# A planned recurrent-attention and gated-MLP kernel: transfers planned in a row, 48-column states, an update of eight products

## The chip, the core and the metric

The kernel runs on one core of a Trainium2 chip. Five engines work side by side and meet through semaphores: PE (TensorE: matmuls, with the weight loads listed apart as PEld), DVE (VectorE), ACT (ScalarE), POOL (GpSimd) and SP, which here does nothing but issue DMA transfers. The metric is the device time of one execution in microseconds; the figure of a kernel is the median of its runs.

## The reference

Four batches of eight heads carry a 48x48 state through 768 steps; the outputs of all heads side by side, 384 numbers for each of 3072 tokens, then go through a gated MLP of 2048 hidden units.

```python
for t in range(S):
    state = alpha[:, :, t, :, None] * state + np.einsum('bhd,bhe->bhde', k[:, :, t], v[:, :, t])
    y[:, :, t] = np.einsum('bhd,bhde->bhe', q[:, :, t], state)
...
h = x @ w_in
sp = np.where(h > 20.0, h, np.log1p(np.exp(np.minimum(h, 20.0))))
g = h * np.tanh(sp)
return (g @ w_out).astype(np.float32)
```

All inputs and the output are float32.

## The kernel before

**Attention.** `attention(n)` (L420 to L667) treats one chunk: 128 tokens of one batch, all eight heads. There are 24 chunks, the four batches in turn for each of six stretches of the sequence, so that chunk n and chunk n+4 share a state. Heads go in four pairs j; the two heads of a pair lie on partitions 0 to 47 and 64 to 111 of q, k and alpha (`R` is 112). DVE makes running products of alpha from the back (`rest`, L471) and from the front (L483) and multiplies them into k (L479) and q (L493). PE then makes the scores of the chunk (`sc`, L507, eight products with 48 rows of weights each), DVE masks them into `probs` (L515), and PE sums in `y` what the state gives (L530, `state` as weights) and what the chunk itself gives (L530, `v` as weights). ACT and DVE split `y` into an upper and a lower fp32r half (`xs`, and `x3` for the last two heads, whose rows six small DMAs then move into place, L576). For the next chunk of the batch PE turns k round (`kb`, L638), ACT copies it (`ks`, L642), PE multiplies it with v (`u`, L647), and DVE adds the diagonal blocks of `u` into the state (L659), which it has decayed first (L498).

The state of a batch holds for each pair a 112x112 block-diagonal tile, with zeros off the diagonal, so one product serves both heads of a pair. Decay and addition touch the two diagonal blocks in two instructions each. The update product makes all 96 columns of a pair, of which half the entries are used.

**MLP.** `unit` (L673 to L796) treats one block f of 128 hidden units for two or four chunks: nine products to `h` (L689), eight passes over 256 or 512 columns on ACT and DVE (L697 to L723) to `g`, and three products per chunk into an output bank `o` (L753). There are 110 units. `weight` unpacks the weights of a block with three DVE passes over `w_lead` (L340, L345, L350) and splits them into `wi` and `wo`; `weight_check` loads every block a second time (`wc`).

**Order.** Nothing of this is ordered by a scheduler: `Plan.order` plays all tasks through with the costs of `COST` and due times (keys), and emits them in that order under a manual schedule. A key is counted in units. A chunk is due `LEAD` units before the first unit that needs it, and at least `SPREAD` units before the next chunk; the weights of block f are due `W_LEAD` units ahead, shifted by `W_SHIFT`. A transfer is a task of SP (some row moves: of ACT) with a time to issue and a fixed time until it has landed, whatever else is in flight. The first `PARTED` chunks load alpha apart from q and k. Until 24 us of the plan, `fill` puts products of 384 columns that nobody reads (`spare`, L804) where the plan sees PE idle. Only what comes before and after the plan, such as the last check on `ok`, `every` and `pf` (L842 to L866), is placed by the framework's own scheduler. After it each engine reads the flag `good` and jumps over the code of `general_path`.

Of the kernel before, what the change touches and what calls it, by code (L numbers as in the profile page):

```python
# [9 lines left out]
F32 = mybir.dt.float32  # L10
F32R = mybir.dt.float32r
BF16 = mybir.dt.bfloat16
I32 = mybir.dt.int32
U32 = mybir.dt.uint32
AF = mybir.ActivationFunctionType
ALU = mybir.AluOpType
# [34 lines left out]
LEAD = 8.0  # L51
SPREAD = 2.0
W_LEAD = 4.0
# [5 lines left out]
CHECK_STEP = 2.0  # L59
FILLS = 150  # L60
IDLE, IDLE_UNTIL, IDLE_BANK = 12.34567, 24.0, "o3"
EARLY_BANKS = {0: ["att", "att", "o0", "o1", "o0"], 1: ["o2", "o1", "att", "o0", "o1"]}
PARTED = 3
DUE_SHIFT = {}
W_SHIFT = {5: -2, 7: -2, 15: -1}
X_PE = 4
# [17 lines left out]
class Task:  # L84
    def __init__(self, engine, cost, late, key, emit, port):
        self.engine, self.cost, self.late, self.key, self.emit = engine, cost, late, key, emit
        self.port = port
        self.needs, self.behind, self.uses, self.begin = [], [], [], None


class Plan:


# [10 lines left out]

    def add(self, engine, cost, late, key, emit, needs=(), uses=(), behind=(), port=False):
        t = Task(engine, cost, late, key, emit, port)
        t.needs, t.uses, t.behind = list(needs), list(uses), list(behind)
# [18 lines left out]
    def order(self):  # L126
# [6 lines left out]
        for e in ENGINES:  # L133
            waiting[e].sort(key=lambda t: t.key)
        done, n, port_free = [], len(self.tasks), 0.0

# [23 lines left out]
        while len(done) < n:  # L160
# [48 lines left out]
COST = {  # L209
    "load part": (0.7, 3.3), "load q": (1.8, 5.0), "load two": (1.2, 4.0), "load v": (0.7, 4.0),  # L210
    "load w": (2.0, 5.0),
    "move": (0.63, 2.5), "store": (0.47, 3.0),
    "fill": (0.165, 0.2), "fill0": (0.33, 0.36),
# [19 lines left out]


def fast_path(ctx, tc, qka, v, w, out, good):
    nc = tc.nc
# [85 lines left out]
    def weight(f):  # L322
# [9 lines left out]

        got = add("SP", *COST["load w"], max(key, FIRST_W + f) - 4, load, uses=[stage])
        fs = slice(f * P, (f + 1) * P)
# [53 lines left out]
    def weight_check(f):  # L388
# [20 lines left out]

        t = add("SP", *COST["load w"], key - 4, load, uses=[again])  # L410
        t = add("ACT", *COST["w check"], key, squares, [t], [again])
# [8 lines left out]
    def attention(n):  # L420
# [27 lines left out]
        if n == 0:  # L448
            got_a, got_k, got_q = (
                add("SP", *COST["load part"], -99 + 0.1 * i, load_part(*e), uses=[q_buf])  # L450
                for i, e in enumerate(((a_at, QKA), (k_at, a_at), (0, k_at)))
            )
        elif n < PARTED:
            got_a, got_k = (
                add("SP", *COST[z], key - Q_LEAD - early, load_part(*e), uses=[q_buf])
                for z, e, early in (
                    ("load part", (a_at, QKA), 1.0), ("load two", (0, a_at), 0.0)
                )
            )
            got_q = got_k  # L460
        else:
            got_a = got_k = got_q = add("SP", *COST["load q"], key - Q_LEAD, load, uses=[q_buf])
        got_v = add("SP", *COST["load v"], key - V_LEAD, load_v, uses=[v_buf])

# [29 lines left out]

        def decay(r):
            def part():
                o = st[r : r + D, :, r : r + D]
                nc.vector.tensor_tensor(  # L498
                    o, o, total()[r : r + D].broadcast_to([D, NPAIR, D]), ALU.mult
                )  # L500
            return part

# [15 lines left out]
        def product():  # L518
            p = new(y_buf, [P, NPAIR, C], f"y{n}", ps)
            ops = []  # L520
            if not first:
                ops += [(p[:R, j], st[:, j], Q()[:, j]) for j in range(NPAIR)]
            for j in range(NPAIR):
# [5 lines left out]
            for m, (o, l, r) in enumerate(ops):  # L529
                nc.tensor.matmul(  # L530
                    o, l, r, start=m < (2 if first else 1), stop=m >= len(ops) - 2,
                    skip_group_check=True,
                )
# [60 lines left out]
        if not first:  # L594
            for i, r in enumerate((0, 64)):
                t_decay.append(
                    add(
                        "DVE", *COST["state"], key + 0.1, decay(r), [t_rest, *done_state[b]],
                        [rest], port=True,
                    )  # L600
                )
        t_sc = add("PE", *COST["scores"], key + 0.2, scores, [t_k, t_q], [q_buf, *sc_buf])
        t_mask = [
# [21 lines left out]
        moved = [  # L625
            add(MOVER(n, s, r), *COST["move"], key + 0.64, move(s, r), [hi3, lo3, hi, lo], [x3])
            for s in range(NK) for r in (0, 64)
# [16 lines left out]
        def update():  # L644
            p = new(u_buf, [P, NPAIR, C], f"u{n}", ps)
            for j in range(NPAIR):
                nc.tensor.matmul(  # L647
                    p[:R, j, : 2 * D], ks_buf.tile[:, j], V()[:, 2 * D * j : 2 * D * (j + 1)],
                    start=True, stop=True,
                )  # L650

        def gather(a, r):
            def part():
                o = st[r : r + D, :, r : r + D]
                u = u_buf.tile[r : r + D, :, a * D : (a + 1) * D]
                if first:
                    nc.scalar.copy(o, u)
                else:
                    nc.vector.tensor_tensor(o, u, o, ALU.add)  # L659
            return part  # L660
# [4 lines left out]
        done_state[b] = [  # L665
            add(
                *(("ACT", *COST["state0"]) if first else ("DVE", *COST["state"])), key + 1.0,  # L667
                gather(a, r), [t_u, t_y, *t_decay], [u_buf],
            )
            for a, r in enumerate((0, 64))  # L670
        ]

# [3 lines left out]
    def unit(c0, nt, f, at, ends):  # L676
# [64 lines left out]
        for j in range(nt):  # L741
# [51 lines left out]
            written = add("ACT", *COST["result"], k, result, done, [osb] if from_part else [o, osb])  # L793
            add("SP", *COST["store"], k, store, [written], [osb])

# [67 lines left out]
    nc.vector.memset(ones, 1.0)  # L863
    pf = ps.tile([1, 3 + n_chunks - n_last], F32, tag="att", name="pf", bufs=BUFS["att"])
    nc.tensor.matmul(pf, ones, every, start=True, stop=True)
    nc.vector.tensor_reduce(good, pf, AX.X, ALU.min)  # L866
# [196 lines left out]
```

## Time and profile before

| what | us |
|---|---|
| median of three runs | 536.36 |
| the three runs | 536.14, 536.36, 539.34 |
| the profiled execution, its own time | 539.41 |
| its span, first to last instruction | 537.6 |

The profile is of a fourth execution. Its span leaves out 1.8 us around the program, and the execution took 0.6% more than the median of the runs; durations below come from it, and the comparison of kernels goes by the medians. In the rows, a `MATMUL` of plain float32 is two instructions, one of fp32r is one, so the four update products of a chunk are eight rows of `u`. A timeline row gives start, length, engine, line, operation, tiles and count; neighbouring instructions of one group stand in one row. Matmuls overlap each other, so the time that a group takes on PE is read from the start of its row to the start of the next. A bracket at a row's end tells how long the engine was idle before it, and who ended that.

### The profile page before, as it was taken

The page shows a single profiled execution, that of the slowest core. Times are in us where ns is not written, and L with a number is a line of the kernel's source. Part 1 is how long each engine was busy: PE and PEld are TensorE (multiplying, and loading weights), DVE is VectorE, ACT ScalarE, POOL GpSimd, SP SyncE. Part 2 cuts the span into 40 slices and gives each one's busy share as a digit, 9 for nine tenths or more (in the row PEclk, how much of TensorE's full clock was granted, in tenths as well). Part 3 has the DMA queues.
Part 4 walks back from the last instruction along what each step waited for, and adds up shares of the span by engine and source line. Part 5 has one row for each costly group of instructions (what it writes and reads, how often), then busy time and mean ns, then how long its engine had stood idle before and what let it go on. Part 6 is the DMA issues. An engine that isn't in the chain of part 4 may idle for free.

```text
span 537.6 us, 9425 instructions
## 1 busy us (share of the span) xinstructions
PE 524.9 (98%) x3392; PEld 467.2 (87%) x3392; DVE 394.3 (73%) x686; ACT 397.4 (74%) x930; POOL 36.0 (7%) x37
## 2 busy tenths in 40 slices
PE   7998999999999999999999999999999999999996
PEld 4688998998898888988899888899988899999996
DVE  8998999999997598678875567885458745554452
ACT  1597787899789797998676855567776577787774
POOL 2003010332440000000000000000000000000000
PEclk9999999999999999999999999999999999999999
DMA  8685243532533668556120132220042000010001
GB/s 262 193 267 176 75 134 83 183 119 65 178 118 121 190 191 268 203 176 199 51 68 1 44 90 75 75 73 1 1 132 76 7 9 1 0 60 1 1 0 62
DMA packets 22067, 54.18 MB, mean 101 GB/s; under 512 B 4033, under 2 KB 14785, under 8 KB 22017
## 3 DMA queue, kind: packets, MB, share of 16 engines
q1 hardware_dynamic: 21728, 53.45, 31.9%
q8 instruction: 27, 0.44, 0.4%
q14 instruction: 24, 0.19, 0.1%
q10 hardware_dynamic: 288, 0.10, 0.1%
HBM read 46.45 MB, written 4.72 MB: 95 GB/s over the span
## 4 chain that ended last, share of the span: by engine, by line
PE 74%; DVE 12%; DMA 6%; ACT 5%; issue 2%; SPq 1%; DVEq 0%; ACTq 0%
PE o L753 30%; PE h L689 30%; PE y L530 7%; PE sc L507 4%; DMA ws<-in_wp_dram 3%; PE u L647 2%; DVE w_lead L345 2%; DVE t L716 2%; PE kb L638 1%; DVE rest L471 1%; DVE g L723 1%; DMA qka<-in_qka_dram 1%; DVE w_lead L350 1%; DVE y L707 1%; DMA xs<-x 1%
## 5 line engine op out<-in xcount | busy, mean ns | idle before, releaser
L753 PE MATMUL o<-wo,g 128*128 128x384 f32 x1152 | 229.2, 342 | 0.6 <-DVE g L723 0.6
L689 PE MATMUL h<-xs,wi 128*128 128x512 f32 (+1 forms) x990 | 219.2, 366 | 0.7 <-DMA xs<-x 0.7
L753 PEld LDWEIGHTS o<-wo,g 128*128 128x128 f32 x1152 | 201.8, 188 | 10.2 <-DVE g L723 1.2
L689 PEld LDWEIGHTS h<-xs,wi 128*128 128x128 f32 x990 | 170.1, 188 | 26.7 <-DMA xs<-x 0.9
L697 ACT ACTIVATE u<-h 128x512 f32<-128x512 f32 (+1 forms) x110 | 59.3, 539 | 86.8 <-PE h L689 86.6
L707 DVE SCALAR_TENSOR_TENSOR y<-u,h 128x512 f32<-128x512 f32 (+1 forms) x110 | 67.4, 615 | 54.2 <-ACT u L697 53.8
L723 DVE TENSOR_TENSOR g<-t,g 128x512 fp32r<-128x512 f32 (+1 forms) x110 | 68.9, 627 | 50.4 <-ACT g L720 50.1
L710 ACT ACTIVATE t<-t,tenth 128x512 f32<-128x512 f32 (+1 forms) x110 | 73.2, 665 | 2.2
L716 DVE SCALAR_TENSOR_TENSOR t<-y,t 128x512 f32<-128x512 f32 (+1 forms) x110 | 69.4, 632 | 4.4 <-ACT t L713 4.4
L720 ACT ACTIVATE g<-t 128x512 fp32r<-128x512 f32 (+1 forms) x110 | 62.4, 567 | 8.2 <-DVE t L716 4.4
L703 ACT ACTIVATE t<-u 128x512 f32<-128x512 f32 (+1 forms) x110 | 63.3, 575 | 5.3 <-DVE g L723 1.9
L713 ACT ACTIVATE t<-t 128x512 f32<-128x512 f32 (+1 forms) x110 | 62.5, 568 | 0.6
L471 DVE TENSOR_TENSOR_SCAN rest<-qka,behind 112x516 f32<-112x516 f32 x24 | 30.3, 1262 | 10.1 <-DMA qka<-in_qka_dram 10.1
L515 DVE COPY_PREDICATED probs<-causal,sc 128x512 f32<-128x512 uint32 x48 | 32.5, 728 | 0.4 <-PE sc L507 0.2
L507 PEld LDWEIGHTS sc<-qka 48*128 48x128 f32 x384 | 23.6, 187 | 8.0 <-issue 3.1
L483 DVE TENSOR_TENSOR_SCAN qka<-qka,ahead 112x516 f32<-112x516 f32 x24 | 30.2, 1259 | 0.0
L507 PE MATMUL sc<-qka 48*128 48x128 f32 x384 | 28.2, 285 | 2.0 <-DVE qka L493 2.0
L366 POOL TENSOR_TENSOR wi<-w_lead,wi 128x384 fp32r<-128x384 f32 x12 | 18.8, 1570 | 122.1 <-ACT wi L363 122.1
L530 PE MATMUL y<-probs,v 128*64 128x128 f32 (+1 forms) x384 | 26.6, 278 | 0.1
L530 PEld LDWEIGHTS y<-probs,v 128*64 128x64 f32 (+1 forms) x384 | 20.5, 129 | 4.1 <-DVE probs L515 1.0
L530 PE MATMUL y<-qka,state 112*112 112x128 f32 x160 | 20.9, 273 | 0.8 <-DVE probs L515 0.8
L697 ACT ACTIVATION_READ_ACCUMULATOR u<-h 128x1 f32 x110 | 21.4, 194 | 0.0
(82 smaller groups left out, 381.9 us busy)
## 6 DMA issues: line engine op xcount, KB each, us to landing
qka<-in_qka_dram SPq DMA_DIRECT2D x21, 674.2 KB, 4.8
ws<-in_wp_dram SPq DMA_DIRECT2D x16, 768.0 KB, 4.6
wc<-in_wp_dram SPq DMA_DIRECT2D x16, 768.0 KB, 4.8
v<-in_vp_dram SPq DMA_DIRECT2D x24, 192.0 KB, 3.4
out_dram<-osb SPq DMA_DIRECT2D x16, 192.0 KB, 1.9
xs<-x SPq DMA_DIRECT2D x138, 16.0 KB, 2.3
out_dram<-part SPq DMA_DIRECT2D x8, 192.0 KB, 3.8
qka<-in_qka_dram SPq DMA_DIRECT2D x2, 448.0 KB, 5.8
```

The source lines that it names most:

```text
L507: nc.tensor.matmul(p[a][:, j], K()[r : r + D, j], Q()[r : r + D, j], start=True, stop=True)
L530: nc.tensor.matmul(o, l, r, start=m < (2 if first else 1), stop=m >= len(ops) - 2, skip_group_check=True,)
L689: nc.tensor.matmul(p[:, :N], wi[:, z, s, fs], x[:, a, s], start=m == 0, stop=m == len(passes) - 1)
L697: nc.scalar.activation(wide(u), wide(h), AF.Exp, scale=-1.0, accum_out=uchk[:, at : at + 1])
L703: nc.scalar.activation(wide(t), wide(u), AF.Square, bias=1.0, scale=2.0)
L707: nc.vector.scalar_tensor_tensor(wide(y), wide(u), 0.5, wide(h), ALU.add, ALU.mult)
L710: nc.scalar.activation(wide(t), wide(t), AF.Ln, bias=tenth, scale=0.1)
L713: nc.scalar.activation(wide(t), wide(t), AF.Exp, scale=-1.0)
L716: nc.vector.scalar_tensor_tensor(wide(t), wide(y), 0.4, wide(t), ALU.mult, ALU.mult)
L720: nc.scalar.activation(g.tile[:, 0, :N], wide(t), AF.Copy)
L723: nc.vector.tensor_tensor(g.tile[:, 1, :N], wide(t), g.tile[:, 0, :N].bitcast(F32), ALU.subtract)
L753: nc.tensor.matmul(o.tile, g.tile[:, a, j * C : (j + 1) * C], wo[:, z, f], start=begins and m == 0, stop=end and m == 2,)
```

## The change

Four things are changed in the code.

1. The state tile is 48 columns wide instead of 112 (allocated with 64, the last 16 zero), both heads of a pair one above the other on partitions 0 to 47 and 64 to 111. The product with q becomes two products per pair, each with 48 rows of weights, into the upper or the lower half of `y`.
2. The update becomes two products per pair, each with its own 48 (or 64) columns of k as weights and 48 columns of v, so eight for a chunk instead of four. Decay and addition are then one instruction each over 112 partitions instead of two over 48.
3. The plan counts a transfer by `MOVES` (issue, transfer, landing): the transfers of all queues go one behind the other through `transfers_free`. `SPREAD` is 2.5 instead of 2, `PARTED` 1 instead of 3, `W_SHIFT` is empty.
4. Ahead of the product for `pf`, 22 products of one column of the identity (`PADS`) are written into the same tile.

```diff
-SPREAD = 2.0
+SPREAD = 2.5
...
+PADS = 22
...
-PARTED = 3
+PARTED = 1
...
-W_SHIFT = {5: -2, 7: -2, 15: -1}
+W_SHIFT = {}
...
+            if t.transfer:
+                transfers_free = max(transfers_free, at + t.cost) + t.transfer
+                t.late += transfers_free - at
...
-    "load part": (0.7, 3.3), "load q": (1.8, 5.0), "load two": (1.2, 4.0), "load v": (0.7, 4.0),
...
+MOVES = {
+    "load part": (0.43, 0.81, 1.6), "load two": (0.43, 1.6, 1.6), "load q": (0.37, 2.4, 1.6),
...
-        t = const.tile([R, NPAIR, R], F32, name=f"state{b}")
+        t = const.tile([R, NPAIR, 64], F32, name=f"state{b}")
...
+    def move_task(name, key, emit, needs=(), uses=(), queue="SP"):
+        issue, transfer, landing = MOVES[name]
+        return add(queue, issue, landing, key, emit, needs, uses, transfer=transfer)
...
-                ops += [(p[:R, j], st[:, j], Q()[:, j]) for j in range(NPAIR)]
+                for j in range(NPAIR):
+                    for r, wide in ((0, 64), (64, D)):
+                        rows = slice(r, r + D)
+                        ops.append((p[r : r + wide, j], st[rows, j, :wide], Q()[rows, j]))
...
-                nc.tensor.matmul(
-                    p[:R, j, : 2 * D], ks_buf.tile[:, j], V()[:, 2 * D * j : 2 * D * (j + 1)],
-                    start=True, stop=True,
-                )
...
+                for a, (r, rows) in enumerate(((0, 64), (64, D))):
+                    h = (2 * j + a) * D
+                    nc.tensor.matmul(
+                        p[r : r + rows, j, :D], ks_buf.tile[:, j, r : r + rows], V()[:, h : h + D],
+                        start=True, stop=True, skip_group_check=True,
+                    )
...
+        def gather():
+            u = u_buf.tile[:R, :, :D]
...
+                nc.vector.tensor_tensor(st[:, :, :D], u, st[:, :, :D], ALU.add)
...
+    for _ in range(PADS):
+        nc.tensor.matmul(pf[:, :1], some[:, :1], some[:, :1], start=True, stop=True)
     nc.tensor.matmul(pf, ones, every, start=True, stop=True)
```

What the new plan and the scheduler make of this is seen in the order of the built programs. Three places matter below.

The first is on PE, among the down products (`o`) and up products (`h`) of units 88 to 91, late in the program. Before:

```order
L753 MATMUL o18_0_4374<-wo_108,g87_4773 128x384 x3
L753 MATMUL o19_0_4380<-wo_108,g87_4773 128x384 x3
L753 MATMUL o16_0_4321<-wo_108,g88_4807 128x384 x3
L689 MATMUL h91_4831<-xs0_109,wi_107 128x512 x9
L753 MATMUL o17_0_4365<-wo_108,g88_4807 128x384 x3
```

After (`pf` is the tile of the last product, `ident` the identity):

```order
L875 LDWEIGHTS ident_69
L875 MATMUL pf_5681<-ident_69 1x1
L760 MATMUL o16_0_4453<-wo_108,g88_4925 128x384 x2
L875 LDWEIGHTS ident_69
L875 MATMUL pf_5681<-ident_69 1x1
L760 MATMUL o16_0_4453<-wo_108,g88_4925 128x384
L696 MATMUL h91_4949<-xs0_109,wi_107 128x512 x9
L760 MATMUL o17_0_4484<-wo_108,g88_4925 128x384 x3
```

The one-column products are not behind the last product: they are in ten such places, one to three in each, between the down products of units 85 to 90, and none stands after the last `o`.

The second is on DVE, early, around the last two running products of chunk 4 and the first pass over the weights of block 5 (`w_lead5` from `ws5`). Before:

```order
L707 SCALAR_TENSOR_TENSOR y2_539<-u2_519,h2_490 128x256
L483 SCALAR_TENSOR_TENSOR qka4_369<-qka4_369,ahead_86 112x516
L340 TENSOR_SCALAR w_lead5_563<-ws5_483 128x768
L493 TENSOR_TENSOR qka4_369<-qka4_369 112x512
L707 SCALAR_TENSOR_TENSOR y3_577<-u3_569,h3_541 128x256
```

After:

```order
L498 SCALAR_TENSOR_TENSOR qka4_392<-qka4_392,ahead_86 112x516
L723 SCALAR_TENSOR_TENSOR t2_502<-y2_545,t2_502 128x256
L508 TENSOR_TENSOR qka4_392<-qka4_392 112x512
L714 SCALAR_TENSOR_TENSOR y3_593<-u3_577,h3_558 128x256
L730 TENSOR_TENSOR g2_586<-t2_502,g2_586 128x256
L512 TENSOR_TENSOR state0_95<-state0_95,rest4_498 112x4x48
```

The pass over `ws5` stood ahead of chunk 4's product with q (L493, now L508); it now comes later, behind the masks of chunk 4.

The third is on DVE between units 39 and 42, around the first scan of chunk 11 and the masks of chunk 10. Before:

```order
L716 SCALAR_TENSOR_TENSOR t41_2200<-y41_2198,t41_2200 128x512
L471 SCALAR_TENSOR_TENSOR rest11_2271<-qka11_2212,behind_88 112x516
L515 COPY_PREDICATED probs0_91<-causal_78,sc10_0_2261 128x512
L515 COPY_PREDICATED probs1_93<-causal_78,sc10_1_2262 128x512
L476 RECIPROCAL ahead_86<-rest11_2271 112x4
```

After:

```order
L730 TENSOR_TENSOR g40_2302<-t40_2213,g40_2302 128x512
L526 COPY_PREDICATED probs0_91<-causal_78,sc10_0_2292 128x512
L526 COPY_PREDICATED probs1_93<-causal_78,sc10_1_2293 128x512
L486 SCALAR_TENSOR_TENSOR rest11_2325<-qka11_2260,behind_88 112x516
L491 RECIPROCAL ahead_86<-rest11_2325 112x4
```

The masks of chunk 10 now come ahead of the scan that needs the load of chunk 11. Elsewhere the two plans run alike: 48 fills in both, the same sets of products up to the first down product, and chunks due up to four units earlier.

More of the change, by code (lines that the diff above doesn't have):

```diff
@@ L14 @@
 U32 = mybir.dt.uint32
+U16 = mybir.dt.uint16
 AF = mybir.ActivationFunctionType
@@ L86, in __init__ @@
         self.engine, self.cost, self.late, self.key, self.emit = engine, cost, late, key, emit
-        self.port = port
+        self.port, self.transfer = port, 0.0
         self.needs, self.behind, self.uses, self.begin = [], [], [], None
@@ L103, in buffer, with add @@
         return made
-    def add(self, engine, cost, late, key, emit, needs=(), uses=(), behind=(), port=False):
+    def add(self, engine, cost, late, key, emit, needs=(), uses=(), behind=(), port=False, transfer=0.0):
         t = Task(engine, cost, late, key, emit, port)
+        t.transfer = transfer
         t.needs, t.uses, t.behind = list(needs), list(uses), list(behind)
@@ L134, in order @@
             waiting[e].sort(key=lambda t: t.key)
-        done, n, port_free = [], len(self.tasks), 0.0
+        done, n, port_free, transfers_free = [], len(self.tasks), 0.0, 0.0
         def ready(t):
@@ L209 @@
 COST = {
-    "load part": (0.7, 3.3), "load q": (1.8, 5.0), "load two": (1.2, 4.0), "load v": (0.7, 4.0),
-    "load w": (2.0, 5.0),
-    "move": (0.63, 2.5), "store": (0.47, 3.0),
     "fill": (0.165, 0.2), "fill0": (0.33, 0.36),
@@ L232 @@
 EXPLORE = None
+MOVES = {
+    "load part": (0.43, 0.81, 1.6), "load two": (0.43, 1.6, 1.6), "load q": (0.37, 2.4, 1.6),
+    "load v": (0.43, 0.7, 1.6), "load w": (0.37, 2.8, 1.4), "move": (0.62, 0.18, 1.2),
+    "store": (0.34, 0.6, 1.0),
+}
 def fast_path(ctx, tc, qka, v, w, out, good):
@@ L331, in load @@
             )
-        got = add("SP", *COST["load w"], max(key, FIRST_W + f) - 4, load, uses=[stage])
+        got = move_task("load w", max(key, FIRST_W + f) - 4, load, uses=[stage])
         fs = slice(f * P, (f + 1) * P)
@@ L408, in tiny @@
             )
-        t = add("SP", *COST["load w"], key - 4, load, uses=[again])
+        t = move_task("load w", key - 4, load, uses=[again])
         t = add("ACT", *COST["w check"], key, squares, [t], [again])
@@ L449, in attention @@
             got_a, got_k, got_q = (
-                add("SP", *COST["load part"], -99 + 0.1 * i, load_part(*e), uses=[q_buf])
+                move_task("load part", -99 + 0.1 * i, load_part(*e), uses=[q_buf])
                 for i, e in enumerate(((a_at, QKA), (k_at, a_at), (0, k_at)))
@@ L454, in attention @@
             got_a, got_k = (
-                add("SP", *COST[z], key - Q_LEAD - early, load_part(*e), uses=[q_buf])
+                move_task(z, key - Q_LEAD - early, load_part(*e), uses=[q_buf])
                 for z, e, early in (
@@ L461, in attention @@
         else:
-            got_a = got_k = got_q = add("SP", *COST["load q"], key - Q_LEAD, load, uses=[q_buf])
-        got_v = add("SP", *COST["load v"], key - V_LEAD, load_v, uses=[v_buf])
+            got_a = got_k = got_q = move_task("load q", key - Q_LEAD, load, uses=[q_buf])
+        got_v = move_task("load v", key - V_LEAD, load_v, uses=[v_buf])
         def scan_rest():
@@ L493, in mult_q, with decay @@
             nc.vector.tensor_tensor(Q(), Q(), front[:, :, 1:], ALU.mult)
[L495 to L499, printed above, removed]
-                )
-            return part
+        def decay():
+            o = st[:, :, :D]
+            nc.vector.tensor_tensor(o, o, total().broadcast_to([R, NPAIR, D]), ALU.mult)
         def scores():
@@ L530, in product @@
                 nc.tensor.matmul(
-                    o, l, r, start=m < (2 if first else 1), stop=m >= len(ops) - 2,
+                    o, l, r, start=m < 2, stop=m >= len(ops) - 2,
                     skip_group_check=True,
@@ L594, in attention @@
         if not first:
[L595 to L600, printed above, removed]
+            t_decay.append(
+                add(
+                    "DVE", *COST["state"], key + 0.1, decay, [t_rest, *done_state[b]], [rest],
+                    port=True,
                 )
+            )
         t_sc = add("PE", *COST["scores"], key + 0.2, scores, [t_k, t_q], [q_buf, *sc_buf])
@@ L625, in attention @@
         moved = [
-            add(MOVER(n, s, r), *COST["move"], key + 0.64, move(s, r), [hi3, lo3, hi, lo], [x3])
+            move_task("move", key + 0.64, move(s, r), [hi3, lo3, hi, lo], [x3], MOVER(n, s, r))
             for s in range(NK) for r in (0, 64)
@@ L646, in update @@
             for j in range(NPAIR):
-                nc.tensor.matmul(
-                    p[:R, j, : 2 * D], ks_buf.tile[:, j], V()[:, 2 * D * j : 2 * D * (j + 1)],
-                    start=True, stop=True,
[L650 to L660, printed above, removed]
+                for a, (r, rows) in enumerate(((0, 64), (64, D))):
[3 more added lines that the diff above has]
+                        start=True, stop=True, skip_group_check=True,
+                    )
+        def gather():
+            u = u_buf.tile[:R, :, :D]
+            if first:
+                nc.scalar.copy(st[:, :, :D], u)
+            else:
+                nc.vector.tensor_tensor(st[:, :, :D], u, st[:, :, :D], ALU.add)
         t_kb = add("PE", *COST["turn"], key + 0.8, turn, [t_k], [q_buf, kb_buf])
@@ L664, in attention @@
         t_u = add("PE", *COST["update"], key + 0.9, update, [t_ks, got_v], [ks_buf, v_buf, u_buf])
[L665 to L671, printed above, removed]
+        kind = ("ACT", *COST["state0"]) if first else ("DVE", *COST["state"])
+        done_state[b] = [add(*kind, key + 1.0, gather, [t_u, t_y, *t_decay], [u_buf])]
     part, kept, sums, downs = {}, {}, {}, {}
@@ L793, in unit @@
             written = add("ACT", *COST["result"], k, result, done, [osb] if from_part else [o, osb])
-            add("SP", *COST["store"], k, store, [written], [osb])
+            move_task("store", k, store, [written], [osb])
     if FILLS:
```

## The prediction

> **What bounds the kernel now.** I read the page first: busy shares, slices, the chain that ended last.
>
> ```profile
> PE 524.9 (98%) x3392; PEld 467.2 (87%) x3392; DVE 394.3 (73%) x686; ACT 397.4 (74%) x930; POOL 36.0 (7%) x37
> PEclk9999999999999999999999999999999999999999
> PE 74%; DVE 12%; DMA 6%; ACT 5%; issue 2%; SPq 1%; DVEq 0%; ACTq 0%
> ```
>
> PE is busy for 98% of the span at full granted clock, and the chain runs through PE for 74% of it; DVE, DMA and ACT share the rest. A busy PE need not be a full PE, so I then read four stretches (columns: PE, PEld, DVE, ACT, POOL busy, clock, DMA share, GB/s).
>
> ```profile
> 0.00:24.50 24.50, 21.07 (x161) 13.83 (x161) 20.90 (x34) 8.80 (x23) 3.53 (x13) 1.00 0.76 232
> 24.50:60.00 35.50, 33.13 (x268) 29.29 (x267) 32.56 (x60) 27.32 (x84) 4.41 (x4) 1.00 0.65 200
> 60.00:532.70 472.70, 470.43 (x2965) 423.94 (x2963) 340.50 (x592) 360.62 (x821) 28.07 (x20) 1.00 0.28 86
> 532.70:537.60 4.90, 0.22 (x3) 0.11 (x2) 0.32 (x2) 0.65 (x4) 0.00 (x0) 0.91 0.46 163
> ...
> L804 PE MATMUL spare<-ident 128*128 128x384 bf16 x48 | 11.1, 374 | 2.8 <-POOL ident masks.py:199 2.8
> ```
>
> Up to 24.5 us DVE sets the pace and PE passes 11.1 us with the 48 fills. From 60 to 532.7 us PE is idle for 2.3 us of 472.7. So from about 60 us on, each microsecond added to or taken from PE's work moves the end by as much; DVE has 132 us to spare there, and fewer DVE instructions are worth nothing by themselves. The timeline of PE over chunk 8 shows what its groups cost.
>
> ```profile
> 131.10 1.75 PE L753 MATMUL o<-wo,g 128*128 128x384 f32 x9
> 132.77 1.16 PE L507 MATMUL sc<-qka 48*128 48x128 f32 x16
> 133.87 0.80 PE L753 MATMUL o<-wo,g 128*128 128x384 f32 x3
> 134.50 2.25 PE L689 MATMUL h<-xs,wi 128*128 128x512 f32 x9
> 136.58 1.75 PE L753 MATMUL o<-wo,g 128*128 128x384 f32 x9
> 138.17 1.04 PE L530 MATMUL y<-qka,state 112*112 112x128 f32 x8
> 139.13 1.09 PE L530 MATMUL y<-probs,v 128*64 128x128 f32 x16
> 140.15 0.60 PE L638 MATMUL kb<-ident,qka 112*128 112x112 f32 x4
> ...
> 202.22 0.93 PE L647 MATMUL u<-v,ks 128*112 128x96 f32 x8
> 202.94 0.78 PE L753 MATMUL o<-wo,g 128*128 128x384 f32 x3
> 203.56 2.22 PE L689 MATMUL h<-xs,wi 128*128 128x512 f32 x9
> ...
> L530 PE MATMUL y<-probs,v 128*64 128x128 f32 x192 | 26.3, 279 | 0.0
> ```
>
> The nine `o` from 136.58 to 138.17 give 0.177 us each. Three things follow. Pairs run side by side: the 16 rows of `y` from `probs`, which alternate between two column halves of the array, start within 1.09 - 0.28 = 0.81 us, so a pair takes 0.11 us, hardly more than the 0.12 us of a single row of the state product (0.96 us for eight). Second, going from products over the whole array to such halves and back costs something: from 131.10 to 134.50 there are 3.40 us, less twelve `o` (2.12 us) 1.28 us, less eight pairs 0.88 us, leaves 0.40 us for going in and out, of which 0.08 us stand ahead (1.67 us for nine `o`). Third, the update does not pay this now: 0.72 us, and the three `o` behind it take 0.62 instead of 0.53, 0.81 us in all.
>
> **The change, part by part.**
>
> *State product.* Eight rows become 16 in eight pairs, each pair on two opposite quarters of the array. Priced as the `probs` group, 1.02 us, with 0.08 us to go in, less the 0.96 us that go: +0.14 us per chunk, and 20 chunks have it, all after 50 us where nothing covers PE: +2.8 us. The trace has no pair of this shape. Bounds: 0 if going between two divided shapes is free, and eight more steps of 0.11 us (+1.02, so +20.4 us) if the two quarters of a pair wait for each other. I take +2.8, since both divided shapes that the trace shows, `sc` by rows and `probs` by columns, run in pairs.
>
> *Update.* Eight rows of 112 weight columns become 16 of 64 or 48, with half the moving columns. The weight loads then set the step:
>
> ```profile
> 54.13 0.19 PEld L530 LDWEIGHTS y<-probs,v 128*64 128x64 f32 x4
> ...
> L530 PEld LDWEIGHTS y<-probs,v 128*64 128x64 f32 x192 | 20.3, 136 | 3.8 <-DVE probs L515 0.6 <-issue 0.4
> ```
>
> Four loads, two in each half, lie in 0.19 us, the last of them 0.14 long, so a second pair begins 0.055 us after the first. Eight pairs at 0.055 and 0.40 to go in and out are 0.84 us against 0.81: +0.03, over the 16 updates that lie behind 50 us +0.5 us. Upper bound: pairs no faster than those of `sc`, 1.28 us, +0.47 each, +7.5 us. Lower: each product half of now's 0.09 us step, -0.06 each, -1.0 us. I take the loads, the nearest row in shape.
>
> *One addition, one decay.* 32 DVE instructions of 0.35 and 40 of 0.39 us become half as many over more partitions. After 60 us DVE's idle time hides both: 0.
>
> *The 22 one-column products.* By the order of the built program they stand in ten places among the `o` of units 85 to 90, not behind the last product. There PE is full, so they are paid. They use one column of weights, a divided shape again, so I charge each place as going in and out.
>
> ```profile
> L753 PEld LDWEIGHTS o<-wo,g 128*128 128x128 f32 x1152 | 201.8, 188 | 10.2 <-DVE g L723 1.2 <-issue 0.7
> ...
> L865 PE MATMUL pf<-every,ones 128*1 128x7 f32 x2 | 0.2, 168 | 1.0 <-DVE every L851 1.0
> L865 PEld LDWEIGHTS pf<-every,ones 128*1 128x1 f32 x2 | 0.1, 80 | 1.3 <-PE o L753 1.3
> ...
> 533.70 0.19 PE L865 MATMUL pf<-every,ones 128*1 128x7 f32 x2 [0.97 <-DVE every L851]
> ```
>
> The load of one column takes 0.08 us against 0.19, so 0.40 - 0.11 = 0.29 us per place, 2.9 us for ten; two rows of `pf` start 0.19 - 0.17 = 0.02 us apart, 22 of them 0.5 us: +3.4 us. Bounds: 0.5 without any going in and out, 5.8 with 0.40 per place and 0.08 per product. The Trainium skill, "TensorEngine Tiling (Array Packing)", Instruction Overhead, gives about 60 cycles for any matmul however few its columns; at 2.4 GHz an estimate from that page is 0.55 us for 22, and the sum would be 2.9 us lower by it. The same page's Key Properties say that a change of tiling mode drains the array, and the 0.40 us of `sc` agrees.
>
> *The plan at the start.* Two waits stand out where PE runs dry after the fills.
>
> ```profile
> 41.02 1.22 DVE L483 TENSOR_TENSOR_SCAN qka<-qka,ahead 112x516 f32<-112x516 f32 x1
> 44.26 0.56 DVE L340 TENSOR_SCALAR w_lead<-ws 128x768 int32<-128x768 int32 x1 [2.02 <-DMA ws<-in_wp_dram]
> 44.73 0.69 DVE L493 TENSOR_TENSOR qka<-qka 112x512 f32<-112x512 f32 x1
> ...
> 42.06 1.75 PE L753 MATMUL o<-wo,g 128*128 128x384 f32 x9
> 45.47 1.23 PE L507 MATMUL sc<-qka 48*128 48x128 f32 x16 [1.67 <-DVE qka L493]
> ...
> 8.00 1.23 DVE L471 TENSOR_TENSOR_SCAN rest<-qka,behind 112x516 f32<-112x516 f32 x1 [0.54 <-DMA qka<-in_qka_dram]
> ```
>
> DVE stood behind the landing of `ws5` with chunk 4's product behind it, and PE with `sc`. That pass now comes later, the product can follow the scan at 42.2, and `sc` can start when the nine `o` are through, 42.06 + 1.59 = 43.65 instead of 45.47: -1.8 us. Against it, chunk 1 comes in one transfer: its alpha, awaited at 8.0, comes with 448 KB more, at the stretch's 232 GB/s 1.9 us later, of which the product moved ahead of it fills 0.6. The fills give that room. I take -1.5, bounds -2.5 and +1.5.
>
> *The plan later.*
>
> ```profile
> 183.85 2.38 PE L753 MATMUL o<-wo,g 128*128 128x384 f32 x12
> 185.02 1.23 DVE L471 TENSOR_TENSOR_SCAN rest<-qka,behind 112x516 f32<-112x516 f32 x1 [2.73 <-DMA qka<-in_qka_dram]
> 186.28 1.34 DVE L515 COPY_PREDICATED probs<-causal,sc 128x512 f32<-128x512 uint32 x2
> 187.06 1.13 PE L530 MATMUL y<-qka,state 112*112 112x128 f32 x8 [0.83 <-DVE probs L515]
> 211.27 2.31 PE L689 MATMUL h<-xs,wi 128*128 128x512 f32 x9 [0.69 <-DMA xs<-x]
> ```
>
> The masks of chunk 10 waited behind a scan whose load had not landed; they now stand ahead of it, so `y` starts at 183.85 + 12 x 0.177 = 185.97 instead of 187.06: -1.0 us. What is late next is the scan of chunk 11, with 1.1 us of slack gained. Of the 0.69 us at 211 I take half, for moves that start earlier: -1.4 us together. Bounds -2.8, and +2 for new waits of this size.
>
> *The end.* Behind the last `o` the same `every`, `pf` and flag follow: 0.
>
> Sum: 2.8 + 0.5 + 3.4 - 1.5 - 1.4 = **+3.8 us**. The profiled execution took 539.41 us, so it would take 543.2; that execution stands 0.6% above the median, and on the median of 536.36 the sum gives **540.2 us**. A measurement of this kernel tells about 1% (5.4 us) from no change.
>
> **The rivals.**
>
> *Update pairs at 0.11 us* (slower): if two loads or two products in the halves cannot follow each other faster than in any pair shown, the update is +0.47 us and the total 547.2. It decides as soon as a pair takes over 0.065 us. For it: nothing in the trace runs pairs faster. Against it: the 0.055 us between loads.
>
> *The quarters serialize* (slower): 540.2 + 17.6 = 557.8. For it: both halves of `sc` have a tile of their own, while two quarters now write one `y` tile from different rows. The Trainium skill, "TensorEngine Tiling (Array Packing)", Restrictions and Gotchas, says that different row tiles cannot access the same PSUM bank at once, which speaks for this rival; no run here shows it yet. Against it: the quarters write different partitions, as the `probs` pairs do.
>
> *The one-column products are nearly free* (no change): 0.5 us instead of 3.4, 537.3.
>
> *The plan gains more* (faster): all waits of PE after the fills gone and 4 us of the 11.1 us of fills saved, 530.5. Against it: as many fills as before, and the same products up to the first `o`.
>
> *New waits*: the weights of blocks 5, 7 and 15 lose their earlier due times, chunks come earlier and want their buffers earlier; two or three waits of 1.67 us, 544.
>
> **How the numbers follow.** The sum as worked out has 0.58; its terms leave 0.43 within 1%, 0.14 slower, 0.01 faster. Pairs at 0.11 us: 0.10, slower. Serial quarters: 0.05, slower. Free one-column products: 0.15, of it 0.13 within 1% and 0.02 faster. More gain: 0.04, faster. New waits: 0.08, of it 0.06 slower. Together 0.07 faster, 0.58 within 1%, 0.35 slower. The predicted time is that of the likeliest, 540.2 us; the range from 535.0 (free one-column products and the larger gains of the plan) to 546.5 (most of the way to slow update pairs) leaves out the serial quarters, the large gain and about half of the slow pairs.
>
> **What would show it.** The state group should take about 1.1 us with 16 rows, the update about 0.75 us to the next row; 2 us in either says that pairs do not overlap. Around units 85 to 90 an `o` next to one-column products should be late by 0.3 us. `sc` of chunk 4 should follow the `o` with no wait, as should the state product of chunk 10. The forecast is wrong if PE's start of full work moves by more than 2 us, or if a divided shape costs other than 0.4 us to enter and leave.

## The result and the profile after

| kernel | median, us | runs | before on the same chip, us | ratio, 95% interval |
|---|---|---|---|---|
| changed | 545.02 | 5 | 538.35 | 1.0119 [1.0082, 1.0156] |
| changed, again | 545.21 | 5 | 539.15 | 1.0127 [1.0105, 1.0149] |
| before, again | 538.84 | 8 | 539.15 | 0.9998 [0.9978, 1.0018] |

The changed kernel is slower by 1.2%, 6 to 7 us. The time of 545.02 us lies in the range given (535.0 to 546.5); the forecast of +3.8 us was a little over half of what came. The forecast time of 540.2 us stood on a median of 536.36 us from three runs; five runs of the kernel before gave 538.35 us, so 2 of the 4.8 us between 540.2 and 545.02 are the base and not the change. The likeliest outcome, a time within 1% of before, had 0.58; 1.2% (interval 0.8 to 1.6) lies with the slower ones, which had 0.35. The profiled execution took 547.44 us. Its page and the four stretches, with the bounds of those of before:

```profile
PE 532.8 (98%) x3734; PEld 460.4 (84%) x3734; DVE 384.3 (70%) x650; ACT 399.4 (73%) x926; POOL 40.1 (7%) x37
PEclk9998999999999999999999999999999999999999
PE 79%; DVE 10%; DMA 4%; ACT 3%; issue 2%; SPq 1%; ACTq 0%; DVEq 0%
```

```profile
0.00:24.50 24.50, 20.05 (x161) 12.41 (x162) 20.00 (x34) 8.09 (x21) 2.88 (x13) 1.00 0.80 234
24.50:60.00 35.50, 32.81 (x294) 27.61 (x292) 31.68 (x54) 25.54 (x74) 4.43 (x3) 0.95 0.58 178
60.00:532.70 472.70, 471.57 (x3236) 412.49 (x3236) 329.39 (x556) 359.87 (x817) 32.76 (x22) 1.00 0.28 87
532.70:545.70 13.00, 8.38 (x49) 7.91 (x47) 3.28 (x9) 5.89 (x15) 0.00 (x0) 0.94 0.19 64
```

PE carries the chain still more (79% instead of 74%), and DVE has less to do (384.3 instead of 394.3 us), which gains nothing. From 60 us on PE is full as before, so what is new must be more time per product, or a later start of the full work. The granted clock of 0.95 between 24.5 and 60 us is new, and belongs to this execution. The timeline of PE over chunk 8 and at the one-column products:

```profile
132.75 1.75 PE L760 MATMUL o<-wo,g 128*128 128x384 f32 x9
134.43 1.08 PE L544 MATMUL y<-qka,state 48*64 48x128 f32 x16
135.45 1.09 PE L544 MATMUL y<-probs,v 128*64 128x128 f32 x16
...
137.45 2.25 PE L696 MATMUL h<-xs,wi 128*128 128x512 f32 x9
139.63 0.67 PE L662 MATMUL u<-v,ks 128*64 128x48 f32 x16
140.22 2.38 PE L760 MATMUL o<-wo,g 128*128 128x384 f32 x12
142.44 2.25 PE L696 MATMUL h<-xs,wi 128*128 128x512 f32 x9
144.53 0.69 PE L760 MATMUL o<-wo,g 128*128 128x384 f32 x3
...
460.80 1.75 PE L760 MATMUL o<-wo,g 128*128 128x384 f32 x9
462.48 0.21 PE L875 MATMUL pf<-ident 128*1 128x1 bf16 x3
462.62 0.62 PE L760 MATMUL o<-wo,g 128*128 128x384 f32 x2
463.17 0.16 PE L875 MATMUL pf<-ident 128*1 128x1 bf16 x1
463.26 0.45 PE L760 MATMUL o<-wo,g 128*128 128x384 f32 x1
463.55 2.25 PE L696 MATMUL h<-xs,wi 128*128 128x512 f32 x9
```

*State product.* The nine `o` end at 132.75 + 9 x 0.177 = 134.34, the next group starts at 135.45: 1.11 us, where it was 0.96. *Update.* Nine undisturbed `h` take 2.09 us (142.44 to 144.53), so 0.09 of the 2.18 us ahead of `u` belong to it; with 0.59 us to the next row, and 2.22 instead of 12 x 0.176 us for the `o` behind, 0.79 us, where the prediction read 0.81; read in this way, twelve undisturbed updates of the kernel before have 0.79 too. *One-column products.* The nine `o` ahead end at 460.80 + 1.59 = 462.39, and to 463.55 there are 1.16 us for two places and three `o` (0.53 us): 0.63 us, 0.31 a place.

### The profile page after: what moved, and what is told of

It is laid out like the page before. It is cut to its first block, busy times and chain, and to the rows that moved or that the text cites. A ratio compares the mean times of both kernels' runs of the same rounds, so it can differ in the third digit from the quotient of the medians.

```text
span 545.7 us, 10071 instructions
## 1 busy us (share of the span) xinstructions
PE 532.8 (98%) x3734; PEld 460.4 (84%) x3734; DVE 384.3 (70%) x650; ACT 399.4 (73%) x926; POOL 40.1 (7%) x37
## 4 chain that ended last, share of the span: by engine, by line
PE 79%; DVE 10%; DMA 4%; ACT 3%; issue 2%; SPq 1%; ACTq 0%; DVEq 0%
PE o L760 32%; PE h L696 31%; PE y L544 7%; PE sc L518 4%; DMA xs<-x 3%; PE u L662 2%; DMA qka<-in_qka_dram 1%; PE kb L651 1%; DVE t L723 1%; DVE g L730 1%; DVE y L714 1%; DVE rest L486 1%; DVE w_lead L360 1%; DVE qka L494 1%; SPq L590 1%
## 5 line engine op out<-in xcount | busy, mean ns | idle before, releaser
L760 PE MATMUL o<-wo,g 128*128 128x384 f32 x1152 | 233.9, 344 | 0.2 <-DVE g L730 0.2
L544 PE MATMUL y<-qka,state 48*48 48x128 f32 (+1 forms) x320 | 21.7, 275 | 0.0
```

The lines of the kernel that those rows point to most:

```text
L544: nc.tensor.matmul(o, l, r, start=m < 2, stop=m >= len(ops) - 2, skip_group_check=True,)
L760: nc.tensor.matmul(o.tile, g.tile[:, a, j * C : (j + 1) * C], wo[:, z, f], start=begins and m == 0, stop=end and m == 2,)
```

## The experiments

In the lag tables below, a kernel's lag at some time is how much later than in another trace PE starts the product that has the same work left behind it. It is worked out from the starts of all matmuls, each counted with its pace in the kernel before (a doubled row half, fills and one-column products nothing).

### One part of the change at a time

The edits: `PADS = 0` in the changed kernel; in the kernel before, point 3 of the change alone, points 1 and 2 alone, and of point 3 only the row of transfers and `MOVES`.

> The changed kernel without the 22 one-column products. Its trace has them in ten places at 0.18 to 0.34 us each, 2.6 us in all, and PE is full there. Theory A (they are paid where they stand): 2.6 us faster than the changed kernel, so about 4 us slower than the kernel before, and the row of work at units 85 to 90 shows no step in the lag behind the kernel before. Rival B (they set how the last instructions fall into PE's instruction fetches, and so pay for themselves): no faster than the changed kernel, 6 to 7 us slower than the kernel before.

> The kernel before with the new plan alone (transfers in a row, SPREAD 2.5, PARTED 1, no W_SHIFT), the old states, update and no one-column products. Theory A (the start costs what the forecast credited): the start loses 2 to 3.7 us and the waits near 186 and 210 us give back 1.5 to 2, so +0.5 to +2 us against the kernel before, with PE's waits at 38 and 45 us as in the changed kernel. Rival B (the plan is neutral, the products carry the whole loss): within 0.3 us of the kernel before. Rival C (forecast as made): -2.9 us.

> The kernel before with the 48-column states, the eight-product update and the single decay and addition, under the old plan. Theory A (each state group costs 0.14 us more, each update the same): +2.7 us. Rival B (the products carry the whole loss of the changed kernel but for the one-column ones): +4 us. Rival C (fewer and narrower DVE instructions shorten the start): below +1.5 us.

> The kernel before with the transfers planned in a row, but SPREAD 2, PARTED 3 and W_SHIFT as before. Theory A (the start is lost by chunk 1's single transfer and by the loads that come earlier): no loss at the start, -1 to +0.5 us. Rival B (the row of transfers alone moves the loads and so the loss): +1 to +3 us, with the same waits at 38 and 45 us as in the changed kernel.

| part | median, us | ratio | us |
|---|---|---|---|
| all but the one-column products | 542.67 | 1.0052 [1.0026, 1.0078] | +2.8 |
| plan alone | 541.41 | 1.0051 [1.0024, 1.0078] | +2.8 |
| states and update alone | 539.45 | 1.0012 [0.9992, 1.0032] | +0.6 |
| row of transfers alone | 542.74 | 1.0070 [1.0044, 1.0097] | +3.8 |

(The last column is the ratio on the 539.4 us of before.) The one-column products cost the difference between 1.0119 or 1.0127 and 1.0052, 3.6 to 4.0 us (each kernel against the one before on its own chip); that they pay for themselves is out. Plan and products one by one come to 3.4 us, both at once to 2.8, the same within the intervals. The plan loses 2.8 us where the forecast had it gain 2.9 (rival C). Its interval, 1.3 to 4.2 us, reaches theory A's 0.5 to 2, but not by theory A's cause: its profile has no wait of PE above 0.4 us between 24 and 60 us. Its lag behind the second profile of before (below) is 0.1 us at 52 us, 2.3 at 115 us, and 3.4 at 220 us, behind a wait of 1.20 us for row moves at 213.66 us. The products came out 2 us cheaper than theory A said (+0.6, interval -0.4 to 1.7), nearest to rival C, though their groups take the same 1.11 us in the trace. The row of transfers alone lost most, so a loss of this size needs no change of SPREAD, PARTED or W_SHIFT (rival B, but with waits between 27 and 30, at 101 and at 141 us instead of 38 and 45).

By their orders, the masks of chunk 10 stand ahead of the scan of chunk 11 in the kernel with the new products under the *old* plan, and behind it in the kernel with the new plan and the old products. So points 1 and 2 of the change moved the masks, and not the new plan. The likely way is that one decay and one addition instead of two of each are fewer tasks on DVE; that was not tried alone.

### Second profiles, one table entry, and the fills

> The changed kernel once more, on one chip with the kernel before and the next kernel. Theory A (products +0.7, plan +2.3, one-column products +2.6 to +3): about 5.5 us over the kernel before. Its second profile tells what of the start belongs to the order and what to one execution: two weight loads in a row stand ahead of the load of chunk 5, so the first scan of chunk 5 should again wait for its load by 1 us or more, and the row moves behind it should come late again; the half clock at 49 to 53 us need not come again. Rival B (the late start was one execution's luck): no wait of that scan, the lag at 44 us below 1 us.

> The kernel before once more, for a second profile. If the waits of PE at 45, 187 and 211 us belong to the order they stand there again within 0.3 us (theory A); if they are one execution's they move or vanish (rival B).

In the second profile of before (538.24 us), the three waits that the forecast meant to remove:

```profile
45.87 1.23 PE L507 MATMUL sc<-qka 48*128 48x128 f32 x16 [1.31 <-DVE qka L493]
...
184.19 2.38 PE L753 MATMUL o<-wo,g 128*128 128x384 f32 x12
186.70 1.13 PE L530 MATMUL y<-qka,state 112*112 112x128 f32 x8
...
209.04 1.16 PE L507 MATMUL sc<-qka 48*128 48x128 f32 x16
210.13 2.37 PE L689 MATMUL h<-xs,wi 128*128 128x512 f32 x9
```

The first stands again, but `ws5` (block 5's weights) is not what holds it here. DVE's pass over `ws5` (L340) starts without a wait, and the pass and the product behind it take 1.24 and 1.48 us instead of 0.56 and 0.69, beside two passes of POOL:

```profile
43.17 1.24 DVE L340 TENSOR_SCALAR w_lead<-ws 128x768 int32<-128x768 int32 x1
44.34 1.48 DVE L493 TENSOR_TENSOR qka<-qka 112x512 f32<-112x512 f32 x1
...
42.59 1.41 POOL L366 TENSOR_TENSOR wi<-w_lead,wi 128x384 fp32r<-128x384 f32 x1 [38.42 <-ACT wi L363]
43.95 1.31 POOL L366 TENSOR_TENSOR wo<-w_lead,wo 128x384 fp32r<-128x384 f32 x1
...
184.64 1.23 DVE L471 TENSOR_TENSOR_SCAN rest<-qka,behind 112x516 f32<-112x516 f32 x1 [2.00 <-DMA qka<-in_qka_dram]
185.91 1.36 DVE L515 COPY_PREDICATED probs<-causal,sc 128x512 f32<-128x512 uint32 x2
```

Of the other two no bracket is left. The second is smaller, not gone: the masks of chunk 10 stand again behind a scan that waits for its load, 2.00 instead of 2.73 us, and `y` starts 0.39 us behind the end of the twelve `o` (184.19 + 2.12 = 186.31) instead of 1.09. So the order makes the wait, and the execution its size. The third is gone. These two places account for 1.4 us between the profiles; the second profile is 0.4 us later at the start, which leaves 1.1.

In the second profile of the changed kernel (545.21 us), PE and then DVE and POOL around chunk 4:

```profile
28.56 1.31 PE L696 MATMUL h<-xs,wi 128*128 128x256 f32 x9 [2.34 <-DMA xs<-x]
47.01 1.16 PE L518 MATMUL sc<-qka 48*128 48x128 f32 x16 [1.14 <-ACT t L717]
...
43.12 2.06 DVE L498 TENSOR_TENSOR_SCAN qka<-qka,ahead 112x516 f32<-112x516 f32 x1
45.10 0.39 DVE L723 SCALAR_TENSOR_TENSOR t<-y,t 128x256 f32<-128x256 f32 x1
45.42 1.49 DVE L508 TENSOR_TENSOR qka<-qka 112x512 f32<-112x512 f32 x1
...
42.98 1.10 POOL L381 TENSOR_TENSOR wi<-w_lead,wi 128x384 fp32r<-128x384 f32 x1 [39.46 <-ACT wi L378]
44.05 2.31 POOL L381 TENSOR_TENSOR wo<-w_lead,wo 128x384 fp32r<-128x384 f32 x1
```

The first up product waits 2.34 us for the row moves. In the first profile it starts at 27.05 us without such a wait; without the one-column products it waits 1.68 us, and with one fill 0.83. `sc` of chunk 4 waits still (1.42 us in the first profile): the page puts it down to ACT, but `sc` needs chunk 4's product with q, which ends at 46.91, just ahead of it. DVE's scan takes 2.06 instead of 1.22 us and the product 1.49 instead of 0.69, while POOL splits a block beside them. In the first profile of before, DVE waited for `ws5` during most of POOL's work; in the second it did not, and was slowed in the same way. The wait of chunk 5's scan, which theory A expected, did not come again, and the kernel lost 6.8 us where theory A said 5.5. The lag of this execution behind the second one of before:

```
until us            52    180    220    430    470    528
lag, us           1.07   2.45   2.07   3.80   6.98   6.99
state groups         0      6      8   19.4     20     20
```

20 x 0.14 us of state products are 2.8, the step at the one-column products 3.2, the start 1.07; all between them comes to nothing. The start's share is made by the wait of the first up product: the lag is 0.4 us at 24 us, 1.8 at 30 us, and 1.1 at 48 us.

> The kernel before with one entry of W_SHIFT left out, that of block 5. Its order puts the pass over block 5 behind the product of chunk 4 and the masks of chunk 10 ahead of the scan of chunk 11, under the old plan and with the old products. Theory A (the two waits of 1.67 and 0.83 us go by the order alone): -2 to -2.8 us. Rival B (the start only moves the wait elsewhere, as in the changed kernel): within 0.7 us. Rival C (slower): a new wait of over 1 us before 60 us.

```diff
-W_SHIFT = {5: -2, 7: -2, 15: -1}
+W_SHIFT = {7: -2, 15: -1}
```

541.17 us, 1.0046 [1.0029, 1.0063]. Rival C, though not before 60 us: `sc` of chunk 4 waits 0.19 us only, and the state product of chunk 10 not at all, and in their place stand

```profile
71.98 0.45 PE L753 MATMUL o<-wo,g 128*128 128x384 f32 x1 [0.78 <-DVE g L723]
114.63 1.34 PE L689 MATMUL h<-xs,wi 128*128 128x256 f32 x9 [1.31 <-DVE y L707]
141.02 1.13 PE L530 MATMUL y<-qka,state 112*112 112x128 f32 x8 [0.85 <-DVE probs L515]
```

Both removals that the forecast counted were had here by one entry, and the kernel lost 2.5 us to waits elsewhere.

> The changed kernel with one fill instead of 48. Theory A (idle stretches of PE halve its granted clock for about 3.4 us, as seen once at 49 us): the granted clock is about half for 10 us or more of the first 40 us, and the end comes 2 to 8 us later. Rival B (the half clock has nothing to do with idle time): full clock throughout, the end within 1 us.

```diff
-FILLS = 150
+FILLS = 1
```

546.20 us, 1.0134 [1.0106, 1.0162]. PE is busy for only 14.46 of the first 24.5 us:

```profile
0.00:24.50 24.50, 14.46 (x112) 10.72 (x113) 19.20 (x32) 6.77 (x17) 2.88 (x13) 1.00 0.73 216
```

The clock column says 1.00, but the trace's record of the clock begins only at 22.5 us (at 7.1 us in the second profile of the changed kernel), and the column counts what is not on record as full. The rows tell more. The scores of one chunk, with one fill and then in the second profile of the changed kernel:

```profile
16.54 2.08 PE L518 MATMUL sc<-qka 48*128 48x128 f32 x16
...
15.13 1.16 PE L518 MATMUL sc<-qka 48*128 48x128 f32 x16
```

From 22.6 us on the rows with one fill have their usual lengths. So theory A is right about the clock: PE ran at about half speed for the first 22.5 us. Rival B is right about the time: the end is within 1 us of the changed kernel's. DVE sets the pace there, and the fills, which keep PE fast early, are worth no more at the end than two runs could show.

### What the plan believes of landings

In the second profile of the changed kernel, the DMA issues of the first 50 us (queue, count, size of each, median us from issue to landing) have for the row moves

```profile
xs<-x SPq DMA_DIRECT2D x18, 16.0 KB, 3.3
xs<-x ACTq DMA_DIRECT2D x6, 16.0 KB, 4.2
```

`MOVES` counts 0.62 + 0.18 + 1.2 = 2.0 us, and the cost table of before had 2.5. With 2.0 the plan puts the first up product ahead of the `y` of chunk 2, and PE waits there for the moves; with 2.5 it stood behind the update of chunk 2.

> The changed kernel without the one-column products, and with the row moves planned to land 1.4 us later (landing 2.6 instead of 1.2 us), near the 3.3 to 4.2 us from issue to landing that the traces show early on. The plan then puts the first up product (unit 0) behind the update of chunk 2 instead of ahead of its y. Theory A (the start is lost because the plan believes the row moves 1.3 us too early): no wait of the first h on the row moves (it was 1.7 to 2.3 us), and 1 to 2 us faster than without this edit, so +1 to +2 us against the kernel before. Rival B (PE's order there does not matter, another wait takes its place): within 0.5 us of the changed kernel without one-column products, +2.8 us against the kernel before.

```diff
-PADS = 22
+PADS = 0
...
-"move": (0.62, 0.18, 1.2),
+"move": (0.62, 0.18, 2.6),
```

Theory A, with more saved than its 1 to 2 us: 539.57 us, 0.9990 [0.9973, 1.0007], against 1.0052 without that number. The first `h` has no wait on the row moves. By the times this one number is worth 3.3 us, and brings the kernel level with the one before though its state products still cost 2.8 us. The wait that it was meant to remove was 1.68 us; where the rest came from is not shown. (Its profiled execution, of 542.89 us, was the slowest of twelve, and shows a wait of 1.81 us at 28 us for `probs` instead, with the clock at half behind it.)

> As the kernel with the later row moves, and with all early loads planned to land as late as the traces have them (parts 2.9, q 2.4, v 2.4, weights 1.6 us after the transfer). Theory A (the nearer the plan's landings are to the measured ones, the fewer waits): no wait of PE above 0.5 us after 24 us, and 0 to +1.5 us against the kernel before, which is what the products cost on PE less what their order gives. Rival B (the plan's order is a matter of luck between near equals): waits of the same sum at other places, +2 to +4 us.

```diff
-PADS = 22
+PADS = 0
...
-"load part": (0.43, 0.81, 1.6), "load two": (0.43, 1.6, 1.6), "load q": (0.37, 2.4, 1.6),
-"load v": (0.43, 0.7, 1.6), "load w": (0.37, 2.8, 1.4), "move": (0.62, 0.18, 1.2),
+"load part": (0.43, 0.81, 2.9), "load two": (0.43, 1.6, 2.6), "load q": (0.37, 2.4, 2.4),
+"load v": (0.43, 0.7, 2.4), "load w": (0.37, 2.8, 1.6), "move": (0.62, 0.18, 2.6),
```

> The kernel before with the new plan (transfers in a row, SPREAD 2.5, PARTED 1, no W_SHIFT) and these later landings, with the old states and update. Theory A: -2 to 0 us against the kernel before, 2.5 us or more faster than the new plan with its own landings. Rival B: waits at other places, +1 to +3 us.

> The kernel before with the new plan and the row moves alone planned to land later, with the old states and update and no one-column products. Theory A (the later row moves save the plan about 3 us, as they did for the new products, where the kernel went from +2.8 to -0.5 us): from the +2.7 us of the plan alone to about -0.5 us, down to -3 us if the 2.7 us that the state products cost on PE come on top of what the new products reached. Rival B (a plan's waits are matched to one set of products): +0.5 to +3 us.

| landings | products | median, us | ratio |
|---|---|---|---|
| moves later | new | 539.57 | 0.9990 [0.9973, 1.0007] |
| all later | new | 543.14 | 1.0052 [1.0032, 1.0073] |
| all later | old | 538.49 | 0.9958 [0.9942, 0.9974] |
| moves later | old | 542.97 | 1.0075 [1.0047, 1.0104] |

The same two tables do opposite things for the two sets of products. With all landings later and the new products there are four waits of 0.63 to 1.70 us after 24 us; with the old products, none above 0.82. With the moves alone later and the old products stand

```profile
73.15 1.10 PE L702 MATMUL h<-xs,wi 128*128 128x256 f32 x7 [1.00 <-POOL wi L379]
...
117.14 1.34 PE L702 MATMUL h<-xs,wi 128*128 128x256 f32 x9 [1.62 <-DVE y L720]
...
228.41 1.02 PE L660 MATMUL u<-v,ks 128*112 128x96 f32 x8 [0.84 <-ACT ks L655]
```

Truer landings do not shorten a plan in general: theory A held for two of the four, rival B for the other two (the last lost 4.0 us, more than rival B's 3). The old products under the new plan with all landings later beat both kernels, the one before by 0.4% and the changed one by some 1.6%. Of the change this version keeps the row of transfers, SPREAD, PARTED and W_SHIFT alone.

## Why the prediction was right, and where it was not

| term | forecast, us | from the pair of second profiles, us |
|---|---|---|
| state product | +2.8 | +2.8 (20 x 0.14) |
| update | +0.5 | 0 (0.79 in either kernel) |
| one-column products | +3.4 | +3.2 (by times 3.6 to 4.0) |
| start | -1.5 | +1.1 |
| plan later | -1.4 | about 0 |
| sum | +3.8 | +7.0 |

**Right: the products.** The `probs` group as the price of a pair on opposite quarters held: 16 rows start within 1.08 - 0.27 = 0.81 us, as those of `probs`, and the group takes 1.11 us, forecast 1.10. The serial quarters (557.8 us) are out. The Trainium skill, "TensorEngine Tiling (Array Packing)", Restrictions and Gotchas, says that different row tiles cannot access the same PSUM bank at once. For two quarters that write different partitions of one `y` tile the 0.81 us say otherwise, and the measurement decides. The update's weight loads allow what was taken, 0.055 us a pair, and it came out 0.05 us a time below the forecast 0.84; pairs at 0.11 us (547.2) are out.

**Right: the one-column products.** The price is the way in and out, not the columns: three in a row start 0.025 us apart, and the ten places come to 3.2 us. That rival (nearly free, 537.3) is out. The 60 cycles for a matmul of the Trainium skill, "TensorEngine Tiling (Array Packing)", Instruction Overhead, agree with the spacing (0.55 / 22 = 0.025 us by the prediction's estimate). The sum by that page, 2.9 us lower, left out the place.

**Wrong: the start.** The step that failed is "the product can follow the scan at 42.2, and `sc` can start when the nine `o` are through, 42.06 + 1.59 = 43.65 instead of 45.47". The product came two instructions behind the scan, and `sc` waited all the same: 1.42 and 1.14 us in the two profiles of the changed kernel, 1.14 without the one-column products and 1.41 with one fill, against 1.67 and 1.31 in the two of before. The step took the landing of `ws5` for what holds `sc`, and that landing was one execution's. In the second profile of before, the pass and the product ahead of `sc` run beside POOL at 2.2 and 2.1 times their durations. In the changed kernel the scan begins at 43.12 instead of 41.96 us, and scan and product run beside POOL at 1.7 and 2.2 times. That POOL is what then holds `sc` is read from these durations; no run kept the two engines apart. So here moving the pass gained PE nothing; under the old plan the same move left `sc` a wait of only 0.19 us (one entry of W_SHIFT), where POOL held up a decay instead. What the start lost came ahead of it: in the second profile the first up product, moved forward by the plan, waits 2.34 us for the row moves, which the term did not look at. (In the first profile it did not wait, and 1.2 us were lost at the wait of 1.18 us at 40.50 us.) The number that set them later was worth 3.3 us by the times. PE's full work starts 1.07 us later in the second profiles, under the 2 us that the prediction named as a sign of being wrong; in the first ones it is about 3 us at 52 us, half of it the halved clock. The single load of chunk 1 was sized about right: in the first profile its scan came at 10.35 instead of 8.00 us (1.9 us forecast), and it cost PE little: between the second profiles the lag at 24 us is 0.4 us.

**Wrong: the plan later.** "`y` starts at 183.85 + 12 x 0.177 = 185.97 instead of 187.06: -1.0 us" counts the wait of one execution in full. It was taken off a median of executions that have less of it: in the second profile of before the same order holds `y` for 0.39 us, and the wait at 211 us is gone. In the changed kernel the state product of chunk 10 follows without a wait in both profiles, as forecast, but losses elsewhere took this back. The step was also put down to the wrong part: the masks came ahead through points 1 and 2, whose fewer DVE instructions were entered as 0 because DVE has time to spare. It has, but other tasks give another order.

**The rivals.** New waits (544) was the case nearest to what happened, given 8 in 100; its causes were the due times of the weights and the buffers, not the row moves. The larger gain of the plan (530.5) is out; what it names, 4.6 us of idle PE behind the fills, of which 2.9 are in the sum already, and 4 us of fills, would give 534.5. That 545.02 us fell within the range owes something to the width left for slow update pairs, which did not occur.

**Open.** Where the new products under the old plan get 2 us back in a typical run: their profiled execution (541.06 us) is 1.6 us over the median, and its lag of 2.85 us at the end is just that of the state products. Whether a plan's order can be forecast: of five plans with one to six numbers changed, each against the kernel that it edits, two came out faster and three did not. State and update were not timed apart; their prices are read from the rows. The one-column products behind the last product, where the code has them, were not tried.

## What to carry to other kernels

Price each new group with the way in and out of its shape, from a row of the same kind; this held here within 0.3 us over 20 state groups and ten places. Take a wait for a gain only if a second profile has it with the same cause, and only after looking who else was running while the engine waited: here `sc` waited in both profiles of before, and not for the same thing. Where a planner orders the work, any edit that adds or removes a task, or changes one cost, moves the order everywhere behind it: forecast that part as a spread around zero (here -2.3 to +4 us), not as the sum of the waits that one wants gone.

## What was not expected of the hardware

The changed kernel's first profiled execution has its clock halved for 3.4 us, in which PE was busy throughout. So has that of the kernel with the later row moves (third row):

```profile
44.00:48.00 4.00, 2.58 (x24) 2.29 (x24) 4.00 (x6) 2.66 (x8) 2.65 (x2) 1.00 0.62 129
49.40:52.80 3.40, 3.40 (x18) 3.27 (x17) 2.83 (x6) 1.81 (x5) 0.00 (x0) 0.54 0.09 36
...
29.30:32.60 3.30, 3.30 (x17) 2.31 (x11) 3.23 (x6) 1.61 (x4) 0.00 (x0) 0.50 0.77 250
```

The first costs about 1.6 us of the 2.2 us by which this execution was longer than the second one, whose mean clock was 1.000; the other about 1.7 of the 3.3 us by which its execution stands above the median of its kernel. Each came after waits of PE. The first:

```profile
40.50 0.31 PE L576 MATMUL y<-x,minus_ident 112*112 112x128 f32 x1 [1.18 <-ACT xs L562]
47.30 1.16 PE L518 MATMUL sc<-qka 48*128 48x128 f32 x16 [1.42 <-ACT t L717]
```

The other came behind the wait of 1.81 us for `probs` at 28.06 us. With one fill, PE was idle for 10 of its first 24.5 us and slow until 22.5 us. So idle time and the half clock go together in these three. But the wait of 2.34 us in the second profile of the changed kernel, and one of 1.70 us at 26.62 us with all landings later, were not followed by it. Which waits set it off stays open.

DVE and POOL held each other up when both worked in SBUF: a scan of 1.22 us took 2.06, a product of 0.69 us 1.49, and POOL's pass, 1.01 us where it runs alone, 2.31. It need not be both, nor always the same one: in the first profile of before, the scan at 69.02 us took 2.03 us beside a POOL pass of 1.06, and the scan at 99.92 us 1.23 us beside a POOL pass of 2.37.
